# First layer of a feed-forward network for two blocks of tokens at once, with streamed sums of weights

## The chip, the core and the metric

The kernel runs on one core of one Trainium2 chip. The metric is the device time of one execution in microseconds (us). The core has five engines that run side by side, each through its own fixed list of instructions: PE (TensorE, the matrix engine; PEld is its loading of weights), DVE (VectorE), ACT (ScalarE), POOL (GpSimd) and SP (SyncE, which here only issues DMA transfers). Semaphores order them among each other.

## What is computed

Attention over 8 batches of 8 heads, 576 positions and 64 dimensions, in which scores more than tau below the largest of their row are dropped; its output, as 4608 tokens of 512 columns, goes through a network with one hidden layer of 2048. All in float32.

```python
scores = scale * np.matmul(q, k.transpose(0, 1, 3, 2))
thresh = np.max(scores, axis=-1, keepdims=True) - tau
scores = np.where(scores >= thresh, scores, -1000000000.0)
attn = softmax(scores)                      # in the reference written out
x = (attn @ v), heads side by side          # 4608 x 512
h = x @ w_in                                # 512 x 2048
out = (h * (1.0 / (1.0 + np.exp(-1.702 * h)))) @ w_out
```

## The kernel before, in words

**Attention.** Two heads make a pair, four pairs a batch, 32 pairs in all (n = 0 to 31). For a pair, PE multiplies keys and queries into scores (`scores`, L571), ACT copies them to SBUF (`keep`, L588), DVE takes maxima (`in_groups`, L594, `over_tiles`, L603), ACT crosses the halves (L613), DVE spreads the maximum (L620, L631) and subtracts it (`sub`, L658), ACT drops what is too small (`mask`, L664) and takes exponentials (`exps`, L668), in five tiles. DVE adds them up (L594 again); the sums are inverted (L742), written to DRAM (`sums_out`, L748), and read back spread over partitions (`sums_in`, L755). PE multiplies with the values (`values`, L679), and `place_x` (L783) writes the product with the inverse sums to a tile `xT` of tokens. From pair 6 on, the values of one pair and the scores of the next are one unbroken stretch of PE, a *run* of 144 recorded instructions. A run starts only when three PSUM buffers of the pool psA are free, and, before the change, when all five tiles of exponentials are there.

**Feed-forward.** The tokens are cut into 18 blocks of 256. Blocks 0 and 1 are computed plainly and together, 256 columns to a matmul (L838, L820). Blocks 2 to 13 use Strassen's scheme in Winograd's form, seven products in place of eight, for both layers. `seven` (L1699) lays the first layer of one block out: each quarter product P1 to P7 (`product1`, L895) is 2 halves of 4 x 2 matmuls with 128 columns, because the tokens of the block are halved (`BLK` 256, `HT` 128). Its left sides are quarters of `w_in` or sums of them, `wc[0..2]`, 1 MB each, made once and kept in SBUF (`w_copy`, `w_plus`, L871 and L875); its right sides are quarters of `xT` or sums of them (`x_sum`, L882). ACT and DVE add the products up (`keep1` L920, `add1` L924) and apply the activation (`silu1` L932). `second` (L1776) does the same for the second layer with 256 columns a matmul (`product`, L1230). Blocks 14 to 17 (`tail_blocks`, L1457) use the scheme twice, two blocks at a time; for that, sums of weights are made ahead, by `extra_sum` (L1015) and `extra2_sum` (L1102) in blocks 4 to 10, and stored in DRAM (L1023, L1110), from where they are streamed in.

**The order of the work.** The kernel plans its own order. Each step is a `task` with an engine, an estimated length, a rank, what it waits for and which buffers it takes and gives back; `run_in_order` (L245) plays the tasks through and writes every engine's instructions in the order in which they start there. Tables of numbers (`EARLY`, `SECOND`, `LATER`, `CV`, `L_RANK`, `W_RANK`) shift the ranks. On PE attention goes ahead of feed-forward as soon as it can start. What comes out is a fixed order; on the chip each engine keeps to it and waits where something is late. DMA transfers are issued by SP in the order of its list, one waiting behind another; a few are issued by POOL: the rows of the first eight pairs, `w_plus` and `t_plus` (L954), all ahead of 275 us.

**Buffers.** `arena2` holds scores, values and query/key tiles; its end, from the seat of `s_m1` on (`spare2`), holds `wc` and the sums of x while `seven` runs. `spare_g` (in `arena`) holds the second layer's sums of activations `s1` and `s2`, and for a moment the sums that `extra_sum` makes. The inverse sums of pairs from 6 on share one buffer, `mb`, with the maxima.

Of the kernel before, what the change touches and what calls it, by code (L numbers as in the profile page):

```python
# [10 lines left out]
FP32 = mybir.dt.float32  # L11
# [6 lines left out]
ALU = mybir.AluOpType  # L18
# [3 lines left out]
P = 128  # L22
# [10 lines left out]
def kernel(  # L33
# [94 lines left out]
    NXT = 5  # L128
    limits = {"psA": 3, "psM": 2, "s_m0": 4, "s_m1": 4, "s_t0": 1, "s_t1": 1, "io": 2, "hs": 2, "osb": 2, "xT": NXT, "mb": 1,
              "raw0": 1, "raw1": 1, "qkT0": 1, "qkT1": 1, "v_m0": 1, "v_m1": 1, "w64_0": 1, "w64_1": 1, "row": 1, "row_s": 1, "rc": 1}  # L130
    for x in ("raw0", "raw1", "qkT0", "qkT1", "mb"):
# [6 lines left out]
        "cross_max": -48.44,  # L138
        "exps": 8.27,
        "in_groups": -20.58,  # L140
        "keep": -91.91,
        "load_qk": -140.68,
        "load_v": -22.28,
        "mask": 10.76,
        "one_row": -86.85,
        "over_halves": -24.87,
        "over_tiles": -88.47,
        "place_x": -38.02,
        "row_in": 3.21,
        "row_out": -7.31,  # L150
        "scores_run": -131.23,
        "spread_max": 29.73,
        "spread_sums": 7.58,
        "sub": -0.95,
# [3 lines left out]
        "turned": -73.29,  # L158
# [3 lines left out]
        "cross_max": 21.33,  # L162
        "cross_sums": 28.0,
        "exps": -7.59,
        "in_groups": 89.35,
        "keep": 7.69,
        "load_qk": -3.13,
        "load_v": 156.87,
        "mask": 62.12,
        "over_halves": -25.79,  # L170
        "over_tiles": 12.47,
        "place_x": -6.25,
        "prep": 141.1,
        "row_in": 11.9,
        "row_out": 159.53,
        "scores_run": -65.52,
        "spread_max": 4.94,
        "sub": 100.98,
        "sums_in": 1.57,
        "sums_out": 102.83,  # L180
        "turn_rows": -12.68,
        "turn_sums": -7.39,
        "values": -29.52,
    }
    LATER = {
        "cross_max": 26.13,
        "cross_sums": -42.19,
        "exps": -10.12,
        "in_groups": -7.73,
        "keep": -14.9,  # L190
        "load_qk": -20.4,
        "load_v": -0.04,
        "mask": -16.94,
        "over_halves": 48.55,
        "over_tiles": -87.61,
        "place_x": -5.16,
        "prep": 102.89,
        "scores_run": -94.88,
        "spread_max": 11.06,
        "sub": 15.63,  # L200
        "sums_in": 16.82,
        "sums_out": 139.32,
        "turn_sums": -0.18,
        "values": 4.3,
# [3 lines left out]
        "cv_low": 87.73,  # L208
        "cv_power": 34.31,
        "cv_power2": 17.48,  # L210
        "cv_round": -2.96,
        "cv_whole": 74.25,
        "load_w": -29.8,
# [6 lines left out]
    TABLES, LOAD = {"exps": 1, "first_act": 1, "silu1": 2, "silu2": 2}, 1.28  # L220
# [144 lines left out]

    def seat(tag, x=0):
        o, size = room[tag][x]
        return arena2[:, o : o + size]
# [18 lines left out]
    def rc_pool(n):  # L387
        return "mb" if n >= SINGLE - 1 else "rc"
# [400 lines left out]
    hidden, acc, ths, osbs = {}, {}, {}, {}  # L789
# [14 lines left out]

    def tanh(j):
        ths[j] = work.tile([P, BANK], FP32, name="th", tag="io", bufs=2)
        nc.scalar.activation(out=ths[j], in_=hidden[j], func=AF.Tanh, scale=GELU_SCALE / 2)
# [80 lines left out]
    places = {}  # L888

# [66 lines left out]
    def quarters(blk):  # L956
        if blk < TAIL:
            return qas
        two_slots = [slot_of[f, blk % 2] for f in range(2)]
        return [[y[:, :, ts(h, HT)] for y in two_slots] for h in range(2)]  # L960
# [35 lines left out]
    assert room["s_m1"][0][0] >= N_G + 9 * BANK  # L996
    extra_rows = [dram.tile([P, 3 * BANK], FP32, name=f"ext{x}", tag=f"ext{x}", bufs=1) for x in range(7)]
    loose, tiles2 = {}, {}

    def loose_io(key):  # L1000
        if key not in loose:
            loose[key] = work.tile([P, BANK], FP32, name="th", tag="io", bufs=2)
        return loose[key]
# [11 lines left out]
    def extra_sum(x, k):  # L1015
        y = left1(x)
        a11, a12, a21, a22 = (y[:, c, ts(f, BANK)] for f in range(2) for c in range(2))
        u1, u2, u4 = (spare_g[:, ts(z, BANK)] for z in range(3))
        o, a, b, op = ((u1, a21, a22, ALU.add), (u2, u1, a11, ALU.subtract), (u4, a12, u2, ALU.subtract))[k]
        nc.vector.tensor_tensor(out=o, in0=a, in1=b, op=op)  # L1020

    def extra_out(x):
        nc.sync.dma_start(out=extra_rows[x], in_=spare_g[:, 0 : 3 * BANK])  # L1023

# [6 lines left out]
    def extra_in(blk, x, k):  # L1031
        if blk == TAIL and x == P2 and "b" not in loose:
            loose["b"] = work.tile([P, NDC, BLK], FP32, name="xT", tag="xT", bufs=NXT).rearrange(
                "p c t -> p (c t)"
            )
# [65 lines left out]

    def extra2_sum(x, k):  # L1102
        y = right2(x)
        b11, b12, b21, b22 = (y[:, ts(c, 4), ts(n, HT)] for c in range(2) for n in range(2))
        u1, u2, u4 = (four(spare_g[:, ts(z, BANK)]) for z in range(3))
        o, a, b = ((u1, b12, b11), (u2, b22, u1), (u4, b21, u2))[k]
        nc.vector.tensor_tensor(out=o, in0=a, in1=b, op=ALU.subtract)

    def extra2_out(x):
        nc.sync.dma_start(out=extra2_rows[x], in_=spare_g[:, 0 : 3 * BANK])  # L1110
# [218 lines left out]
    W_RANK = (-72.29, -7.42, 1.49, 46.38, 3.78, 10.04)  # L1329
# [40 lines left out]
    def first_blocks():  # L1370
        xs = list(placed.values())[-NPAIR:]
        for j in range(NFC):
# [7 lines left out]
            a = task("ACT", 0.48, FIRST, tanh, j, after=ffn[-1:], take=("io",))  # L1380
            gelus[j] = task("DVE", 0.59, FIRST, gelu_0, j, after=[a], give=("psM", "io"))
# [56 lines left out]
    queued = {"ch": [], "p5": []}  # L1438
# [337 lines left out]
    def second(blk, ready, sums, minus):  # L1776
# [4 lines left out]
        for x, p in order:  # L1781
# [19 lines left out]
            if p in (0, 2):  # L1801
                continue
# [279 lines left out]
```

## Time and profile before

| | |
|---|---|
| median of 3 runs (lowest, highest) | 1248.26 us (1247.51, 1250.88) |
| the profiled execution: its time, its span | 1251.82 us, 1250.0 us |
| mean granted clock of PE | 0.998 |
| read from and written to DRAM | 86.28 MB, 20.60 MB |

The span is the time from the first to the last instruction in the profile; some 2 us of the execution lie around it. In a line of the profile, L908 is line 908 of the kernel above; `out<-in` are the program's names of tiles, then partitions and tile shape, and `x32` the number of instructions that stand together or were grouped. PE's float32 matmul is recorded as two instructions, so the counts of the profile are twice those of the program. Start times count from the start of the span. A group's "mean ns" on PE contains the overlap of pipelined matmuls: pace is read from start to start or as busy time over count.

### The profile page before, as it was taken

The numbers are of one execution on the slowest core, as the hardware profiler recorded it, in microseconds if no ns is written. First come the engines' busy times: TensorE is split into PE (matmuls) and PEld (weight loads), VectorE is DVE, ScalarE is ACT, GpSimd is POOL, SyncE is SP. The second block draws the span as 40 slices with busy tenths as digits, with TensorE's granted clock in tenths as the row PEclk, the third lists the DMA queues.
The fourth block names the chain that finished last, engine by engine and source line by source line (L and its number), as shares of the span: only waits on it lengthen the run. The fifth ranks groups of instructions, "written<-read, shape, count | busy, mean of one in ns | idle before, by whom it ended". The sixth has DMA issues, their size and how long they took to land.

```text
span 1250.0 us, 27210 instructions
## 1 busy us (share of the span) xinstructions
PE 1222.6 (98%) x11264; PEld 1005.3 (80%) x11264; DVE 1085.7 (87%) x1683; ACT 827.7 (66%) x1209; POOL 32.6 (3%) x59
## 2 busy tenths in 40 slices
PE   8979999999999999999999999999999999999998
PEld 6636854487888888887979788888888897999998
DVE  6989997779879998999898998989788789999796
ACT  6999988786766766676767667667667586330430
POOL 0000012110000000000000000000000000000000
PEclk9999999999999999999999999999999999999999
DMA  8724458781313332223323241422221212344443
GB/s 244 189 68 112 140 126 140 145 152 43 72 39 97 68 91 66 79 65 74 92 57 99 46 116 42 116 49 66 44 71 22 64 45 72 114 120 140 144 121 100
DMA packets 187180, 117.05 MB, mean 94 GB/s; under 512 B 145392, under 2 KB 155632, under 8 KB 186928
## 3 DMA queue, kind: packets, MB, share of 16 engines
q1 hardware_dynamic: 179776, 103.93, 31.6%
q0 software_dynamic: 6592, 11.09, 5.1%
q8 instruction: 88, 1.44, 0.5%
q10 hardware_dynamic: 688, 0.30, 0.1%
q14 instruction: 36, 0.29, 0.1%
HBM read 86.28 MB, written 20.60 MB: 85 GB/s over the span
## 4 chain that ended last, share of the span: by engine, by line
PE 74%; DVE 12%; ACT 10%; DMA 3%; issue 1%; POOL 0%; SPq 0%; DVEq 0%; ACTq 0%; POOLq 0%
PE ops L1230 24%; PE hps L908 14%; PE ps L908 10%; PE pv L679 9%; PE ps L571 9%; ACT arena L668 3%; PE hps L1074 3%; DVE arena L1091 2%; ACT arena L664 2%; ACT arena L588 2%; PE ps L1074 2%; PE ps L1191 2%; DVE arena L1149 2%; PE ops L1191 1%; DVE part L594 1%
## 5 line engine op out<-in xcount | busy, mean ns | idle before, releaser
L594 DVE TRANSPOSE_TENSOR_REDUCE part<-arena 128x36 f32<-128x1152 f32 x300 | 365.8, 1242 | 62.4 <-ACT arena L588 50.0
L588 ACT COPY arena<-ps 128x576 f32<-128x576 f32 x288 | 170.6, 642 | 93.3 <-PE ps L571 93.2
L664 ACT ACTIVATE arena<-arena 128x1152 f32<-128x1152 f32 (+1 forms) x160 | 165.8, 1060 | 56.9 <-DVE arena L658 56.9
L668 ACT ACTIVATE arena<-arena,shift,scl 128x1152 f32<-128x1152 f32 (+1 forms) x160 | 196.6, 1247 | 1.9
L658 DVE TENSOR_TENSOR arena<-arena 128x1152 f32<-128x1152 f32 (+1 forms) x158 | 189.2, 1228 | 1.2 <-DMA arena<-row 0.3
L571 PE MATMUL ps<-arena 64*64 64x288 f32 x2304 | 171.5, 409 | 6.2 <-ACT arena L588 6.1
L1230 PE MATMUL ops<-w_out,arena 128*128 128x256 f32 x768 | 175.8, 382 | 0.0
L1230 PEld LDWEIGHTS ops<-w_out,arena 128*128 128x128 f32 x768 | 143.3, 190 | 27.3 <-issue 9.2
L679 PE MATMUL pv<-arena 64*64 64x288 f32 x2176 | 159.2, 405 | 0.0
L571 PEld LDWEIGHTS ps<-arena 64*64 64x64 f32 x2304 | 83.1, 133 | 66.9 <-ACT arena L588 25.7
L1230 PE MATMUL ops<-arena 128*128 128x256 f32 x576 | 128.5, 379 | 0.0
L679 PEld LDWEIGHTS pv<-arena 64*64 64x64 f32 x2176 | 80.8, 133 | 53.5 <-issue 7.7
L1230 PEld LDWEIGHTS ops<-arena 128*128 128x128 f32 x576 | 109.3, 190 | 15.3 <-issue 0.4
L908 PE MATMUL hps<-xT,w_in 128*128 128x128 f32 x768 | 89.7, 275 | 0.0
L908 PEld LDWEIGHTS hps<-xT,w_in 128*128 128x128 f32 x768 | 88.6, 192 | 1.1 <-issue 0.5
L927 DVE TENSOR_TENSOR arena<-ps,arena 128x512 f32<-128x512 f32 x72 | 46.9, 679 | 44.0 <-PE ps L908 41.3
L922 ACT COPY arena<-hps 128x512 f32<-128x512 f32 x72 | 41.4, 575 | 39.4 <-PE hps L908 39.3
L838 PE MATMUL hps<-xT,w_in 128*128 128x256 f32 x256 | 56.1, 380 | 0.0
L820 PE MATMUL ops<-w_out,arena 128*128 128x512 f32 x128 | 55.9, 595 | 0.0
L838 PEld LDWEIGHTS hps<-xT,w_in 128*128 128x128 f32 x256 | 48.4, 190 | 7.8 <-issue 0.9
L1088 ACT COPY arena<-hps 128x512 f32<-128x512 f32 x38 | 22.2, 583 | 47.7 <-PE hps L1074 47.7
L613 ACT ACTIVATE other<-red,minus_gap 32x18 f32<-32x18 f32 x118 | 36.2, 307 | 25.0 <-DVE red L603 23.4
(211 smaller groups left out, 1773.3 us busy)
## 6 DMA issues: line engine op xcount, KB each, us to landing
arena<-in_v_dram SPq DMA_DIRECT2D x128, 144.0 KB
arena<-exu SPq DMA_DIRECT2D x42, 256.0 KB
arena<-ext SPq DMA_DIRECT2D x39, 256.0 KB
out_dram<-osb SPq DMA_DIRECT2D x32, 256.0 KB
arena<-in_q_dram SPq DMA_DIRECT2D x112, 72.0 KB
arena<-in_k_dram SPq DMA_DIRECT2D x112, 72.0 KB
arena<-row_s SPq DMA_DIRECT2D x48, 144.0 KB
w_out<-in_moe_w_in_dram SPq DMA_DIRECT2D x12, 512.0 KB
```

The costliest lines, as they stand in the source:

```text
L571: nc.tensor.matmul(ps[ts(c, KT), h, 0:SH], lhsT=mats[n, 1][ts(h, D), ts(j, KT)], rhs=mats[n, 0][ts(h, D), ts(c, SH)], start=True, stop=True,)
L588: nc.scalar.copy(out=sT[n, t][:, u], in_=pss.pop((n, j))[:, :, 0:SH])
L594: nc.vector.tensor_reduce(out=stats[n, op][:, t * 2 * QB : min(2 * t + 2, NK) * QB], in_=sT[n, t].rearrange("p u h (g d) -> p (u h g) d", ...
L658: engine.tensor_tensor(out=s, in0=s, in1=mbs[n].unsqueeze(1).to_broadcast(list(s.shape)), op=ALU.subtract)
L664: nc.scalar.activation(out=s, in_=s, func=AF.Prelu, alpha=STEEP)
L668: nc.scalar.activation(out=s, in_=s, func=AF.Exp, scale=scl, bias=shift)
L679: nc.tensor.matmul(o[c][ts(h, D), 0:SH], lhsT=left(j, h)[ts(c, KT)], rhs=sT[n, t][ts(c, KT), u, h, :], start=(j == 0), stop=(j == NK - 1),)
L820: nc.tensor.matmul(acc[i], lhsT=g0[:, j, ts(i, P)], rhs=w_out[:, j, :], start=(j == 0), stop=(j == NFC - 1),)
L838: nc.tensor.matmul(hidden[j][:, ts(i, BLK)], lhsT=w_in[:, c, ts(j, P)], rhs=xTs[i][:, c, :], start=(c == 0), stop=(c == NDC - 1),)
L908: nc.tensor.matmul(o[:, ts(j, HT)], lhsT=left[:, c, ts(4 * y + j, P)], rhs=right[:, c, :], start=(x in (P1, P2, P5) and j + c == 0), stop= ...
L1074: nc.tensor.matmul(o[:, ts(j, HT)], lhsT=left[:, ts(j, P)], rhs=right, start=(m in (P1, P2, P5) and j == 0), stop=(j == 3), skip_group_che ...
L1230: nc.tensor.matmul(banks[blk][k][:, ts(o, HM)], lhsT=left[:, j, :], rhs=right[:, j, :], start=(j == 0), stop=(j == HF - 1),)
```

## The change

Blocks 7 and 8, 9 and 10, 11 and 12 get their first layer together (`seven4`): the scheme's two halves of tokens are then two whole blocks of 256, so each matmul has 256 columns instead of 128, and a product is four quarters of 2 x 2 matmuls, two quarters at a time. The second layer stays as it was, block after block. The larger tiles take the room of `wc`: the three sums of weights are copied to DRAM (`keep_wc`, SP) after block 2's weights are ready, fetched in 256 KB pieces by POOL into four turns of `spare_g` (`w_flow`), and copied back whole before block 13 (`sums_back`), which is done by `seven` again. A fifth turn waits until the first has been used.

The sums for the tail are made in blocks 3 to 6 (eight of them, in a tile of `xT`) and in 7, 9 and 11 (six, through the one buffer `scrap`, each addition waiting for the store before it). `xT` has six buffers instead of five, and the activation's tile of blocks 0 and 1 and some tail tiles come from that pool. Inverse sums of pairs 16 to 27 get a buffer of their own, `rc2`. A run of the pairs after 16 may begin when two of the five tiles of exponentials are there; each further tile is waited for inside the run. The tables of rank shifts have new numbers. A function `alone` for a block 8, 10 or 12 by itself is added too; no block uses it.

```diff
-    NXT = 5
+    NXT = 6
+    SECOND_RC = 4 * NPAIR
     def seat(tag, x=0):
+        if tag == "rc2":
+            return spare2[:, ds(N_G + 4 * BANK, S)]
...
     def rc_pool(n):
+        if SECOND_RC <= n < NP - NPAIR:
+            return "rc2"
         return "mb" if n >= SINGLE - 1 else "rc"
...
+    WIDE = 7
+    WIDE_AT = (7, 9, 11)
+    g1 = spare2[:, 0:N_G].rearrange("p (f j t) -> p f j t", f=2, t=BLK)
+    scrap = spare2[:, ds(N_G + 3 * BANK, BANK)]
...
+    def keep_wc(x):
+        for c in range(2):
+            nc.sync.dma_start(
+                out=wrows[x].rearrange("q p (c f) -> p c q f", c=2)[:, c],
+                in_=wc[x][:, c, :].rearrange("p (q f) -> p q f", q=4),
+            )
...
+    def w_in_turn(k):
+        return spare_g[:, ts(k % 4, BANK)]
+
+    def w_flow(k, x, q):
+        nc.gpsimd.dma_start(out=w_in_turn(k), in_=wrows[WC_OF[x]][q])
...
+    def product4(blk, q, x, k):
+        y = q % 2
+        b11, b12, b21, b22 = (xTs[blk + h][:, ts(d, 2), :] for d in range(2) for h in range(2))
+        right = (b11, b21, x3[1], b12, x3[2], x3[0], b22)[x]
+        if x in WC_OF:
+            left = w_in_turn(k).rearrange("p (c f) -> p c f", c=2)
+        else:
+            left = left1(x)[:, :, ts(q, 2 * P)]
...
+        o = bank1(x, y)
+        for j in range(2):
+            for c in range(2):
+                nc.tensor.matmul(
+                    o[:, ts(j, BLK)], lhsT=left[:, c, ts(j, P)], rhs=right[:, c, :],
+                    start=(x in (P1, P2, P5) and j + c == 0), stop=(j + c == 2),
+                    skip_group_check=True,
+                )
...
+    def scrap_out(second, x, k):
+        nc.sync.dma_start(out=(extra_rows, extra2_rows)[second][x][:, ts(k, BANK)], in_=scrap)
...
+    EARLY_EXTRAS = {
+        3: ((0, P6), (0, P5)), 4: ((0, P3), (0, P1)), 5: ((0, P2), (1, P1)), 6: ((1, P2), (1, P6)),
+    }
+    LATE_EXTRAS = {7: ((0, P4), (1, P4)), 9: ((0, P7), (1, P7)), 11: ((1, P5), (1, P3))}
...
+    def seven4(blk):
...
+        freed = last1 + (kept_wc + list(extra_out_done.values()) if first else [])
...
+        for second_layer, x in LATE_EXTRAS[blk]:
+            for k in range(3):
+                a = task("DVE", 0.6, FIRST, scrap_sum, second_layer, x, k, after=freed + [t_ready[-1], a])
+                a = task("SP", 0.55, FIRST, scrap_out, second_layer, x, k, after=[a], take=RING[0])
+                a = transfer("DMS", 1.4, a, 2, give=RING[0])
...
+        flow_users = {k: ffn[-1:] if k > 1 else last5[-1:] for k in range(4)}
...
+        for (q, x), k in turn.items():
+            if k >= 4:
+                tasks[ready[q, x][0]][5].append(users[k - 4])
...
+            second(blk + h, {P1: both(0, h), P2: both(1, h), P4: both(1, h)}, sums, minus)
...
+    BEGUN = 2
...
-            elif next_blk >= FIRST7:
+            elif next_blk - 1 in WIDE_AT:
+                seven4(next_blk - 1)
+            elif next_blk == TAIL - 1:
+                sums_back()
+                seven(next_blk)
...
+            elif next_blk >= FIRST7 and next_blk not in WIDE_AT:
                 seven(next_blk)
...
-                    after=exped[m] + [loaded[m], pq, pk] + after if t == 0 else [a],
+                    after=exped[m][: BEGUN if n > SECOND_RC else NKT + 1] + exped[m][NKT + 1 :] + [loaded[m], pq, pk] + after
+                    if t == 0 else [a, exped[m][t]],
```

More of the change, by code (lines that the diff above doesn't have):

```diff
@@ L1379, in first_blocks @@
                 ))
-            a = task("ACT", 0.48, FIRST, tanh, j, after=ffn[-1:], take=("io",))
-            gelus[j] = task("DVE", 0.59, FIRST, gelu_0, j, after=[a], give=("psM", "io"))
+            a = task("ACT", 0.48, FIRST, tanh, j, after=ffn[-1:], take=("io",) + (("xT",) if j == 0 else ()))
+            gelus[j] = task("DVE", 0.59, FIRST, gelu_0, j, after=[a],
+                give=("psM", "io") + (("xT",) if j == NFC - 1 else ()),
+            )
         plain1[:] = ffn[-1:]
@@ L1491, in tail_blocks @@
                     after=[extra_out_done[x]] + ([a, placed[NP - NPAIR]] if where == "b" else []),
-                    take=RING[0] + (("xT", "io", "io") if where == "b" and k == 1 else ()),
+                    take=RING[0] + (("xT", "xT") if where == "b" and k == 1 else ()),
                 )
@@ L1774, with sums_back @@
+    def sums_back():
+        outs = list(extra_out_done.values()) + list(extra2_out_done.values())
+        a = None
+        for x in (P6, P5, P3):
+            after = ffn[-1:] + [a] + (last1 + outs if x == P3 else [])
+            a = task("SP", 1.1, FIRST, back_wc, WC_OF[x], after=after, take=RING[0])
+            wc_back[x] = transfer("DMS", 5.6, a, 2, give=RING[0])
+            w_done[{P6: 1, P5: 0, P3: 3}[x]] = wc_back[x]
+    last5, seated = [], []
     T_OF = {P6: 2, P7: 4, P4: 3, P5: 1}
```

449 lines of the change are left out of this document (348 added, 101 removed).

## The prediction

> **What bounds the kernel now.** I read the page's first part, then the busy time by stages, then the order of TensorE's instructions in time, and last what stands just ahead of the attention runs.
>
> ```profile
> PE 1222.6 (98%) x11264; PEld 1005.3 (80%) x11264; DVE 1085.7 (87%) x1683; ACT 827.7 (66%) x1209; POOL 32.6 (3%) x59
> ```
>
> TensorE is busy for 98% of the span. Where the other 27 us lie is told by two stages, from the first block of the seven-product kind to the last of them, and from there to the end (columns: length, then busy time and count for PE, PEld, DVE, ACT, POOL, then clock, DMA share, GB/s):
>
> ```profile
> 256.00:1057.00 801.00, 801.00 (x7343) 675.71 (x7342) 700.59 (x1002) 551.05 (x793) 3.10 (x2) 1.00 0.28 69
> 1057.00:1250.00 193.00, 185.38 (x1645) 179.90 (x1643) 166.60 (x362) 54.35 (x105) 0.00 (x0) 1.00 0.42 126
> ```
>
> In the first stage, which holds blocks 2 to 13, TensorE has no gap at all in 801 us, at full clock. In the tail it lacks 193.0 - 185.4 = 7.6 us, so about 27.4 - 7.6 = 20 us are lost ahead of 256 us. The change works inside the first stage. There a wait taken away gains nothing, because none reaches TensorE; only fewer or faster matmuls gain, and every new wait of TensorE costs its full length.
>
> A busy engine need not be at its best pace, so the pace is read from starts:
>
> ```profile
> 1020.84 3.74 PE L908 MATMUL ps<-xT,arena 128*128 128x128 f32 x32
> 1024.42 7.07 PE L1230 MATMUL ops<-w_out,arena 128*128 128x256 f32 x32
> 1031.33 1.89 PE L1230 MATMUL ops<-arena 128*128 128x256 f32 x8
> ```
>
> The 32 first-layer instructions of 128 columns (two to one float32 matmul of the program) take 1024.42 - 1020.84 = 3.58 us, or 111.9 ns each; the 32 of 256 columns take 1031.33 - 1024.42 = 6.91 us, or 215.9 ns each. Two of 128 columns cost 223.8 ns and one of 256 does the same work in 215.9.
>
> **The change part by part.** *Matmuls.* Blocks 7 to 12 run their first layer as three pairs. A block has 7 products of 2 halves of 4 x 2 matmuls, 112 matmuls in two pairs of halves or 224 recorded instructions; a whole block by itself agrees:
>
> ```profile
> 850.00:900.00 50.00, 25.17 (x224) 25.17 (x224) 1.00 0.23 53
> 550.00:600.00 50.00, 24.87 (x112) 21.04 (x112) 1.00 0.32 82
> ```
>
> (first row line L908 alone, second line L1230 alone). Six blocks are 1344 instructions of 128 columns, which become 672 of 256. The saving is 672 x (223.8 - 215.9) = **5.3 us**. Its bounds: by the whole-stage rows a pair costs 2 x 25.17/224 = 224.7 ns and a 256 one 24.87/112 = 222.1, breaks for attention included, which leaves 672 x 2.7 = 1.8 us. I take 5.3, since the first layer of the plain blocks is the same form with the same weights and holds the pace over its whole run:
>
> ```profile
> L838 PE MATMUL hps<-xT,w_in 128*128 128x256 f32 x256 | 56.1, 380 | 0.0
> ```
>
> 56.1/256 = 219 ns, its breaks included. TensorE's second layer, attention and tail are the same instructions as before.
>
> *Streamed weight sums.* The three summed weights (1 MB each) are copied to DRAM once after block 2 has made them, come back in 36 pieces of 256 KB on GpSimd's queue, twelve to a pair of blocks, and whole before block 13. No row shows such a piece; the nearest are smaller and larger transfers of the same queue (last number: median us to landing):
>
> ```profile
> arena<-row_s POOLq DMA_DIRECT2D x8, 144.0 KB, 5.1
> arena<-w_out POOLq DMA_DIRECT2D x3, 1024.0 KB, 9.9
> ```
>
> So a piece lands 5.1 to 9.9 us after its issue; I take 5.6, near the 144 KB row. GpSimd's issue is bounded by
>
> ```profile
> 250.18 1.24 POOL L877 DMA_DIRECT2D arena<-w_in  x1 [1.09 <-PE ps L571]
> ```
>
> at 1.24 us each, and nothing else is on that queue by then. The first piece of a pair may start when the P5 product of the block before has read its buffer. Behind that stand P3 and the four tasks of P1 and P2: six tasks of 8 x 215.9 = 1.73 us, 10.4 us of cover against 1.2 + 5.6 = 6.8. The later ones reuse a buffer after P6 and are read at P3: seven tasks, 12.1 us, and in the new order of instructions an attention run stands between as well. Cost 0; at the upper end, 1.2 + 9.9 = 11.1, TensorE would wait 0.7 us a pair, 2 us in all.
>
> *Copies out and back.* Six issues on SP for each direction. Back, they wait for block 12's last product; block 13's P1 (16 matmuls, 3.6 us), an attention run and P2 (3.6 us) stand in the new order ahead of P6, which needs the first of them, 16 us; a 1 MB transfer took 9.9. Cost 0, and 1 us if three share the queue. On the way out they stand in SP's queue ahead of the q and k loads of two later head pairs, in a stretch where the DMA engines are already busy:
>
> ```profile
> 250.00:300.00 50.00, 49.97 (x440) 41.18 (x433) 40.92 (x63) 35.56 (x55) 4.34 (x3) 1.00 0.66 120
> ```
>
> 3 MB at 120 GB/s are 25 us of that queue; the loads are for a run a whole interval (28 us or more, below) on. Cost 0 to 2 us, I take 0.
>
> *Sums for the tail.* The same 42 additions and the same bytes as before, but in 34 stores instead of 14; the last 18 sums share one buffer, so each addition waits on VectorE for the store before it, and behind it waits whatever VectorE has next. Before, SP stood waiting for them and TensorE did not:
>
> ```profile
> SPq L1110 <- DVE arena L1107: 48.4, 7, 9.6
> ```
>
> Cost 0 as long as VectorE has room (third rival).
>
> *x sums.* Eight VectorE subtractions of 256 columns a pair of blocks become four of 512:
>
> ```profile
> L886 DVE TENSOR_TENSOR arena<-xT,arena 128x256 f32<-128x256 f32 x24 | 10.0, 418 | 0.1
> L1107 DVE TENSOR_TENSOR arena<-arena 128x512 f32<-128x512 f32 x9 | 6.1, 677 | 0.2
> ```
>
> 8 x 0.42 - 4 x 0.68 = 0.6 us less a pair on VectorE, hidden under TensorE: 0. ScalarE's copies and SiLUs keep count and size; its program has 32 table loads instead of 28.
>
> *Own buffer for the reciprocal sums; runs begun after two of five exponentials.* Both can only start attention runs sooner. TensorE has no gap there, so they are worth 0 by themselves. But they are needed. Before, runs come at 28.1 and 39.5 us by turns, the long turn holding the first layer:
>
> ```profile
> 646.10 2.09 ACT L668 ACTIVATE arena<-arena,shift,scl 128x1152 f32<-128x1152 f32 x2
> 649.01 1.20 PE L679 MATMUL pv<-arena 64*64 64x288 f32 x16
> 679.86 0.87 ACT L668 ACTIVATE arena<-arena,shift,scl 128x576 f32<-128x576 f32 x1
> 688.53 1.20 PE L679 MATMUL pv<-arena 64*64 64x288 f32 x16
> ```
>
> The run at 649.01 starts 0.8 us after its last exponential ends (648.2). The next one's exponentials end at 680.7, 31.7 us after that start, and have 7.8 us to spare. In the new order two runs in a first layer of a pair stand 14 tasks (24.2 us) and a run (9.0) apart, 33.2 us: 1.5 us to spare, plus what beginning early gives. The scores' copies of the run stand behind the exponentials on ScalarE and three PSUM buffers hold the scores, so a run can go on some 3.4 us (seven of its eighteen half-microsecond steps) without the last exponential. Cost 0, with 4.9 us of margin in place of 7.8.
>
> *Start and tail.* The new order of TensorE up to the first seven-product block differs only by two matmuls on the other side of a run, and the tail's by where the last run of values stands (after its first instead of its fourth product) and small swaps. The tail's gaps are 7.6 us; I take no change, and 1.5 us either way.
>
> **Sum.** The profiled execution took 1251.8 us (span 1250.0); less 5.3 gives 1246.5. It lies 3.6 us above the median of the runs, 1248.3; measured against that, 1248.3 - 5.3 = **1243.0 us**.
>
> **Rivals.** *The pace of the new matmuls is that of the broken stage.* Saving 1.8 us, 1246.5. For it: the stage rows; against it: unbroken runs of 215.9 ns with two kinds of weights.
>
> *The change hides its gain behind late weights.* VectorE is busy almost without a break in the short interval:
>
> ```profile
> 620.90:649.00 28.10, 28.10 (x233) 21.95 (x232) 27.81 (x40) 19.32 (x26) 0.00 (x0) 1.00 0.15 36
> 649.00:688.50 39.50, 39.50 (x393) 34.86 (x392) 33.02 (x50) 27.07 (x42) 0.00 (x0) 1.00 0.39 104
> L594 DVE TRANSPOSE_TENSOR_REDUCE part<-arena 128x36 f32<-128x1152 f32 x300 | 365.8, 1242 | 62.4 <-ACT arena L588 50.0
> ```
>
> If GpSimd can write a transfer's descriptors only between two VectorE instructions, the issue waits up to one of 1.24 us. With the slowest landing that is 1.24 + 1.2 + 9.9 = 12.3 against 10.4: 2 us on each of three pairs, 6 us, 1249. Against it: at 250.18 GpSimd issued in 1.24 us beside VectorE. The Trainium skill ("SBUF — State Buffer", the box on the "DVE blocks DMA" trap) speaks against this change at this place: while VectorE runs an instruction that takes both ports, GpSimd cannot write descriptors, with 620 ns growing to about 3100 in its example. By that page's 2.5 us instead of 1.24 the estimate would be 3.2 us a pair, some 10 us, and no gain.
>
> *VectorE and ScalarE fall behind in the pairs (the other side).* A block takes VectorE 27.81 + 33.02 = 60.8 of 67.6 us; two blocks 121.7 of the 133.4 us that a pair then lasts, so 11.7 us are free. Six of the one-buffer sums fall in each pair. In the new order as few as three VectorE rows, some 3 us, stand between two of them; with a store that lands like the 5.1 us row and half a microsecond of issue each sum waits 2.6 us, 16 us a pair. That is 4 us over what is free, and two of the four table loads added fall in the same stretches:
>
> ```profile
> L668 ACT ACT_TABLE_LOAD x13 | 16.7, 1283 | 0.2
> ```
>
> 4 + 2 x 1.28 = 6.6 us a pair, 20 us in all less the 5.3 gained: 1263. It decides from 11.7 us of waits a pair on; up to there it costs nothing, and at 16 it makes the kernel slower even without the loads (3 x 4.3 = 13 against 5.3: 1256). For it: margins of 4.9 us in place of 7.8; against it: no sum made VectorE wait long enough before to reach TensorE.
>
> **How the numbers follow.** The forecast has 0.60; its own range is 1241.5 to 1244.5 by start and tail. The broken pace has 0.12 (1246.5); late weights 0.08 (1245 to 1249); VectorE behind 0.15 (1250 to 1263); 0.05 is for a gain over 7 us by a better start or tail. This kernel's measurement can tell about 0.3%, 3.7 us, from no change: faster is below 1244.5, slower above 1252.0. Faster: 0.52 of the forecast's 0.60, and 0.05 of the larger gain, with 0.03 from the mixed cases, 0.60. Slower: 0.13 of the last rival, 0.01 of late weights, 0.14. Same: 0.26. The range of 1239.5 to 1252.5 leaves out the worse part of the last rival and the end of the larger gain.
>
> **What would show it.** The 256-column first-layer rows at 216 ns from start to start and 672 of them; still no gap of TensorE between 256 us and the tail, the tail starting near 1052; no wait of TensorE on the streamed weights; runs in the pairs about 33 us apart. Wrong would be: TensorE waiting at product P6 for a DMA, at a run's later tiles for ScalarE's exponentials, or VectorE waiting on the stores of its sums for more than 11.7 us a pair.

## The result, and the profile after

Measured in alternation on one chip, the changed kernel takes 1245.13 us (median of 8 runs, 1244.32 to 1245.79) and the kernel before 1250.32 us (8 runs, 1247.51 to 1251.22). The ratio is 0.9958, with a 95% interval of 0.9949 to 0.9967: faster by 0.42%, or 5.2 us. The forecast was 1243.0 us from a median of 1248.3, a ratio of 0.9958 too; the 2.1 us between 1243.0 and 1245.13 are the other median of the kernel before. The profiled execution took 1244.32 us (span 1242.5). Of the 7.5 us between the two profiled executions some 2.3 are chance, since the one of before lay 1.5 us above its median and the one of after 0.8 below.

In the kernel after, the lines have moved: scores L577, values L685, score copies L594, exponentials L674, maxima and sums L600, `place_x` L789, first layer of one block L918, of a pair of blocks L1060 (`product4`), second layer L1354, the tail's first layer L1208 with its additions L1225 and its x sums L1180, its second layer L1315, the streamed pieces L1037 (`w_flow`).

The page's first part and two stages of the profile after (length, then busy time and count for PE, PEld, DVE, ACT, POOL, then clock, DMA share, GB/s):

```profile
PE 1218.3 (98%) x10592; PEld 979.3 (79%) x10592; DVE 1083.4 (87%) x1671; ACT 827.8 (67%) x1213; POOL 52.0 (4%) x95
```

```profile
256.00:1052.40 796.40, 795.91 (x6652) 650.03 (x6651) 697.69 (x990) 553.33 (x802) 22.59 (x38) 1.00 0.35 89
...
1052.00:1242.50 190.50, 184.33 (x1643) 179.36 (x1641) 166.48 (x363) 50.89 (x101) 0.00 (x0) 1.00 0.43 126
```

TensorE has 11264 - 10592 = 672 instructions fewer, as it should. The middle stage still has next to no gap (0.5 us in 796); the tail now has 6.2 us of them instead of 7.6. The stretch of a pair's first layer, in order of time (start, duration, and the number of instructions that stand together):

```profile
636.32 3.72 PE L1060 MATMUL ps<-arena,arena 128*128 128x256 f32 x16
639.88 3.62 PE L1060 MATMUL hps<-xT,w_in 128*128 128x256 f32 x16
643.33 3.62 PE L1060 MATMUL hps<-arena,w_in 128*128 128x256 f32 x16
646.78 3.62 PE L1060 MATMUL ps<-xT,arena 128*128 128x256 f32 x16
650.24 7.07 PE L1354 MATMUL ops<-w_out,arena 128*128 128x256 f32 x32
```

From start to start, 16 instructions take 3.45 us, 216 ns each: the forecast pace. The first row holds 0.1 us more (3.56); an attention run ends just ahead of it.

Adding up all of TensorE's starts by stage, each instruction counted until the next one starts, splits the 7.5 us of the two profiles:

| stage | before | after | difference |
|---|---|---|---|
| start, up to the first seven-product block | 256.37 | 253.55 | -2.82 |
| first layer of blocks 7 to 12 (before: half of that of blocks 2 to 13) | 150.55 | 147.41 | -3.14 |
| second layer of blocks 2 to 13 | 294.45 | 293.36 | -1.09 |
| attention in the middle stage | 205.83 | 207.52 | +1.69 |
| tail, to the end of the span | 192.25 | 190.06 | -2.19 |

(The other half of the first layer, 150.55 us before and 150.60 after, is not in the table.) The start varies from one execution to the next: it takes 253.5 to 255.1 us in the profiles of experiments 1, 2 and 4, which have the changed kernel's buffers and tables there, and 254.1 and 255.5 us in two variants of the kernel before (experiment 6). So its 2.8 us cannot be told from chance. The other stages repeat: from the first seven-product block to the tail it is 801.4 us in the kernel before and in both its variants of experiment 6, and 798.9 to 799.0 us in the changed kernel, in that of experiment 2 and in the changed kernel with the old order of the tail.

The gain of the wide matmuls is the second and third row together, 4.2 us: six of the attention runs that used to interrupt the second layer, about 0.2 us each, interrupt the wide first layer now, which moves 1.1 us from one row to the other. The other 1.1 of the 5.3 us are five short stops in the wide layer (at 609.6, 744.9, 746.8, 878.7 and 880.7 us, 0.17 to 0.28 us each), where a weight load waits for a copy or an addition of the products before it (L1101 and L1106 below). The waits of TensorE's weight loads, in the middle stage of the profile after (total us, times, longest):

```profile
PEld ps L577 <- ACT arena L594: 12.3, 35, 0.6
...
PEld ps L1060 <- ACT arena L594: 2.2, 5, 0.4
PEld hps L1060 <- ACT arena L1101: 1.0, 3, 0.4
...
PEld ps L1060 <- DVE arena L1106: 0.8, 2, 0.4
```

and the same of before:

```profile
PEld ps L571 <- ACT arena L588: 7.7, 23, 0.4
```

The waits of the scores (L577) on the score copies are longer and more frequent. Four runs, at 415.76, 446.05, 551.47 and 1024.14 us, hold 1.4 of attention's 1.7 us: they take 9.2 to 9.4 us where no run of the middle stage before took more than 8.97, and their weight loads wait 0.6 to 1.3 us for score copies. The five waits of L1060 on score copies stand behind attention runs and belong to the breaks. A weight load overlaps the matmul before it, so such totals are more than what TensorE loses.

### The profile page after: what moved, and what is told of

The parts are those of the page before. It is cut to its first block, busy times and chain, and to the rows that moved or that the text cites. A ratio compares the mean times of both kernels' runs of the same rounds, so it can differ in the third digit from the quotient of the medians.

```text
span 1242.5 us, 26030 instructions
## 1 busy us (share of the span) xinstructions
PE 1218.3 (98%) x10592; PEld 979.3 (79%) x10592; DVE 1083.4 (87%) x1671; ACT 827.8 (67%) x1213; POOL 52.0 (4%) x95
## 4 chain that ended last, share of the span: by engine, by line
PE 71%; ACT 16%; DVE 8%; DMA 2%; issue 1%; SPq 0%; POOL 0%; ACTq 0%; DVEq 0%
PE ops L1354 23%; PE ps L577 9%; PE pv L685 9%; PE hps L1060 7%; PE ps L1060 5%; ACT arena L674 4%; PE hps L850 4%; ACT arena L670 4%; PE hps L918 3%; PE hps L1208 3%; PE ps L918 3%; ACT arena L594 3%; DVE arena L1225 2%; PE ps L1208 2%; PE ps L1315 2%; DVE arena L1273 2%
## 5 line engine op out<-in xcount | busy, mean ns | idle before, releaser
L600 DVE TRANSPOSE_TENSOR_REDUCE part<-arena 128x36 f32<-128x1152 f32 x300 | 364.9, 1240 | 64.6 <-ACT arena L594 49.1
L594 ACT COPY arena<-ps 128x576 f32<-128x576 f32 x288 | 170.6, 642 | 104.6 <-PE ps L577 104.4
L674 ACT ACTIVATE arena<-arena,shift,scl 128x1152 f32<-128x1152 f32 (+1 forms) x160 | 195.4, 1247 | 1.8
L577 PE MATMUL ps<-arena 64*64 64x288 f32 x2304 | 171.6, 409 | 5.8 <-ACT arena L594 5.4
L1354 PE MATMUL ops<-w_out,arena 128*128 128x256 f32 x768 | 174.6, 381 | 0.1
L1354 PEld LDWEIGHTS ops<-w_out,arena 128*128 128x128 f32 x768 | 144.2, 190 | 25.6 <-issue 5.7
L685 PE MATMUL pv<-arena 64*64 64x288 f32 x2176 | 160.2, 407 | 0.0
L577 PEld LDWEIGHTS ps<-arena 64*64 64x64 f32 x2304 | 81.2, 132 | 69.4 <-ACT arena L594 31.5
L685 PEld LDWEIGHTS pv<-arena 64*64 64x64 f32 x2176 | 81.3, 133 | 53.8 <-issue 9.1
L1354 PE MATMUL ops<-arena 128*128 128x256 f32 x528 | 118.1, 379 | 0.0
L1354 PEld LDWEIGHTS ops<-arena 128*128 128x128 f32 x528 | 100.2, 190 | 14.0 <-issue 0.4
L850 PEld LDWEIGHTS hps<-xT,w_in 128*128 128x128 f32 x256 | 48.4, 190 | 7.8 <-issue 1.3
L1222 ACT COPY arena<-hps 128x512 f32<-128x512 f32 x38 | 22.2, 584 | 48.1 <-PE hps L1208 48.1
L832 PEld LDWEIGHTS ops<-w_out,arena 128*128 128x128 f32 x128 | 24.1, 190 | 30.1 <-issue 29.8
L918 PEld LDWEIGHTS hps<-xT,w_in 128*128 128x128 f32 x384 | 44.3, 192 | 0.7 <-issue 0.5
L918 PE MATMUL hps<-xT,w_in 128*128 128x128 f32 x384 | 44.8, 275 | 0.0
L1037 POOL DMA_DIRECT2D arena<-wrow x36 | 19.5, 541 | 599.5 <-DVE arena L664 301.7
```

Source lines behind the costliest of these rows:

```text
L577: nc.tensor.matmul(ps[ts(c, KT), h, 0:SH], lhsT=mats[n, 1][ts(h, D), ts(j, KT)], rhs=mats[n, 0][ts(h, D), ts(c, SH)], start=True, stop=True,)
L594: nc.scalar.copy(out=sT[n, t][:, u], in_=pss.pop((n, j))[:, :, 0:SH])
L600: nc.vector.tensor_reduce(out=stats[n, op][:, t * 2 * QB : min(2 * t + 2, NK) * QB], in_=sT[n, t].rearrange("p u h (g d) -> p (u h g) d", ...
L674: nc.scalar.activation(out=s, in_=s, func=AF.Exp, scale=scl, bias=shift)
L685: nc.tensor.matmul(o[c][ts(h, D), 0:SH], lhsT=left(j, h)[ts(c, KT)], rhs=sT[n, t][ts(c, KT), u, h, :], start=(j == 0), stop=(j == NK - 1),)
L832: nc.tensor.matmul(acc[i], lhsT=g0[:, j, ts(i, P)], rhs=w_out[:, j, :], start=(j == 0), stop=(j == NFC - 1),)
```

## The experiments

All medians and ratios of this part are against runs of the kernel before on the same chip, in alternation with it.

**1. Is it the pace?** The changed kernel with each wide matmul issued as two of 128 columns.

```diff
-                nc.tensor.matmul(
-                    o[:, ts(j, BLK)], lhsT=left[:, c, ts(j, P)], rhs=right[:, c, :],
+                for t in range(2):
+                    nc.tensor.matmul(
+                        o[:, ds(j * BLK + t * HT, HT)], lhsT=left[:, c, ts(j, P)], rhs=right[:, c, ts(t, HT)],
...
```

> The changed kernel in which each 256-column matmul of the pairs is issued as two of 128 columns; everything else (streamed weights, buffers, ranks, begun runs) stays. If the pace of the matmuls is the gain, the first layer of blocks 7 to 12 goes from 147.4 us back to 150.5 and the breaks stay: 672 x 7.9 ns = 5.3 us longer, 1250.4 us, ratio 1.000 to the kernel before. If the new order around them is the gain (the tail's gap of 2 us that is gone, and the start), most of it stays: 1247 us or less, ratio 0.9975 or less.

Measured: 1249.87 us (11 runs), ratio 1.0000 (0.9991 to 1.0009). In time order (its L1061 is the pairs' first layer):

```profile
642.52 3.74 PE L1061 MATMUL hps<-xT,w_in 128*128 128x128 f32 x32
646.10 3.74 PE L1061 MATMUL hps<-arena,w_in 128*128 128x128 f32 x32
```

The same work takes 3.58 us where the wide form takes 3.45, and by starts the pairs' first layer is back at 151.5 us against 147.4. All the rest of the change is still in this kernel, and it gains nothing: the pace is the net gain. Whether the wide form is faster in the matmul or because it needs half the weight loads (the 1344 of this kernel against 672) is not shown, since both change together. (Its attention in the middle stage, +1.7 us, and its tail, -2.2 us, both moved as in the changed kernel, and nearly cancel.)

**2. Do the streamed weights come in time?** Each 256 KB piece is fetched twice, one behind the other.

```diff
-        nc.gpsimd.dma_start(out=w_in_turn(k), in_=wrows[WC_OF[x]][q])
+        for _ in range(2):
+            nc.gpsimd.dma_start(out=w_in_turn(k), in_=wrows[WC_OF[x]][q])
```

> The changed kernel with every 256 KB piece of the weight sums fetched twice into the same place (72 transfers instead of 36). If the cover of 10.4 us holds as reckoned, a piece that lands 3.0 us after an issue of 0.54 us, done twice in a row, is still there in time: 1245 us, ratio 0.996, no wait of TensorE on it. If the weights are late already and only just hidden, each pair of blocks loses about 3 us: 1254 us, ratio 1.003.

Measured: 1244.25 us (5 runs), ratio 0.9955 (0.9942 to 0.9967), no slower than the changed kernel. Its middle stage, and then its row of DMA issues (number, size, median us to landing):

```profile
256.00:1052.00 796.00, 795.53 (x6653) 649.65 (x6652) 696.90 (x988) 553.84 (x802) 41.63 (x74) 1.00 0.39 101
```

```profile
arena<-wrow POOLq DMA_DIRECT2D x72, 256.0 KB, 3.1
```

GpSimd is busy nearly twice as long (41.6 us in place of 22.6), and TensorE still lacks only 0.5 us. So the rival of late weights falls.

**3. Are begun runs worth nothing?** The changed kernel with runs planned only when all five tiles of exponentials are there.

```diff
-    BEGUN = 2
+    BEGUN = NKT + 1
```

> The changed kernel in which a run waits for all five tiles of exponentials again. The planner puts the runs elsewhere: the last values come some 12 us of feed-forward work later than in the changed kernel. If early starts are worth nothing by themselves because TensorE always has other work, the stage of blocks 2 to 13 keeps its length and the whole is 1245 to 1247 us, ratio 0.996 to 0.9975. If the pairs need the early start, TensorE gets gaps at the runs or at the tail's start: over 1250 us, ratio over 1.000.

Measured: 1288.67 us (4 runs), ratio 1.0308 (1.0293 to 1.0322). "Worth nothing" fell by far: 43 us. TensorE's instructions in time, with the idle time ahead and who ended it:

```profile
975.45 0.72 PE L577 MATMUL ps<-arena 64*64 64x288 f32 x8
984.94 1.23 PE L685 MATMUL pv<-arena 64*64 64x288 f32 x6 [8.78 <-ACT arena L674]
...
996.09 1.24 PE L577 MATMUL ps<-arena 64*64 64x288 f32 x8 [6.03 <-ACT arena L594]
997.10 2.14 PE L685 MATMUL pv<-arena 64*64 64x288 f32 x16
999.02 2.15 PE L577 MATMUL ps<-arena 64*64 64x288 f32 x16
...
1092.86 1.20 PE L685 MATMUL pv<-arena 64*64 64x288 f32 x16 [3.94 <-ACT arena L674]
1097.98 4.13 PE L685 MATMUL pv<-arena 64*64 64x288 f32 x40 [3.92 <-ACT arena L674]
1111.72 2.05 PE L1208 MATMUL hps<-arena 128*128 128x128 f32 x8 [9.60 <-DVE arena L1180]
```

The instructions themselves wait for the same data as before; the switch acts only through the plan. In the first pair of blocks two runs now stand 50.8 us apart (592.99 and 643.75) where the changed kernel has 35.2, so attention falls behind by part of a run; it is made up by two runs back to back at 967 us, the second of which stands waiting for its exponentials, and by last values 13.6 us into the tail. By starts, attention takes 367.0 us in place of 326.2 and that is 41 of the 43 us.

**4. Is the own buffer of the reciprocal sums needed?** `rc2` is taken away, so the sums share `mb` again.

```diff
     def rc_pool(n):
-        if SECOND_RC <= n < NP - NPAIR:
-            return "rc2"
         return "mb" if n >= SINGLE - 1 else "rc"
```

> The changed kernel in which the inverse sums of pairs 16 to 27 share the buffer of the maxima again. If the own buffer only starts runs sooner, it is worth nothing: 1245 us, ratio 0.996. If the shared buffer holds the maxima of the next pair back long enough to reach TensorE, 2 us or more: 1247 us or more, ratio over 0.9975.

Measured: 1253.27 us (7 runs), ratio 1.0026 (1.0016 to 1.0037): 8 us lost, and more than the gain. **And if all runs are begun early?** The changed kernel with begun runs from pair 9 on:

```diff
-                    after=exped[m][: BEGUN if n > SECOND_RC else NKT + 1] + exped[m][NKT + 1 :] + [loaded[m], pq, pk] + after
+                    after=exped[m][: BEGUN if n > SINGLE + 1 else NKT + 1] + exped[m][NKT + 1 :] + [loaded[m], pq, pk] + after
```

> The changed kernel with begun runs for all unbroken runs from pair 9 on, not only after pair 16; it computes all. Theory (where TensorE has no gap an earlier run is worth nothing, and it pays only where the next exponentials are the last to come): 1245, within 1.5 us. Rival A (a run begun early waits inside itself for its later exponentials, and those waits are TensorE's): slower by 0.5 us or more a run, 8 runs, 1249 or more. Rival B (it also draws attention out of the tail, as the kernel without begun runs pushed it in): 1240 to 1243.

Measured: 1255.46 us (5 runs), ratio 1.0043 (1.0029 to 1.0056). The time is in Rival A's range, but not for its reason: the eight runs that now may begin early, at 281.63 to 512.58 us, take 8.96 to 8.97 us each, so none of them waits inside. The time is lost in runs behind them, at 619.97 to 930.41 us, which may begin early in the changed kernel too and do not wait there. Both kernels lose the same 9 us in attention (335.2 us in each, against 326.2). TensorE's waits in the middle stage, first without `rc2` (its lines are two lower), then with all runs begun:

```profile
PE pv L683 <- ACT arena L672: 5.8, 3, 1.9
```

```profile
PE pv L685 <- ACT arena L674: 3.9, 2, 1.9
PE ps L577 <- ACT arena L594: 2.3, 4, 0.7
PE hps L918 <- ACT arena L932: 1.1, 1, 1.1
```

In both, the pairs' runs stand unevenly: 26.4, 31.8, 36.0 and 42.9 us apart with all begun (697.45, 723.88, 755.72, 791.75, 834.64), where the changed kernel has 31.6 to 35.2. The run at 755.72 comes 58.3 us after the last but one, waits, and takes 11.45 us in place of 8.97; without `rc2` the run at 756.63 does the same after 58.3 us. In the changed kernel two intervals are never under 65 us there, and no run of the pairs waits. This fits a chain of maxima, masks and exponentials that needs more than 58.3 us for two pairs; that chain was not changed by itself.

**5. Are the new numbers of the planner's tables part of it?** The changed kernel with all the old numbers (one of some 80 lines):

```diff
     LATER = {
-        "cross_max": 86.38,
+        "cross_max": 26.13,
...
```

> The changed kernel with the old tables of rank shifts (EARLY, SECOND, LATER, CV, L_RANK, W_RANK); it computes all. Theory (the gain is the pace of 672 matmuls, and the tables only keep the order such that nothing is late): in the planned order the runs now come irregularly and the last run of values stands 11.6 us of feed-forward work later in the tail, as it also did in the kernel without begun runs, so it loses: 1255 to 1270. Rival (the new numbers are worth nothing, since TensorE has no gap ahead of the tail): 1245, as the changed kernel, within 2 us. Second rival (the new numbers are the gain): about 1250.

Measured: 1269.34 us (4 runs), ratio 1.0155 (1.0141 to 1.017). And the kernel before with all the new ones, the same lines the other way round:

> The kernel before with the new tables of rank shifts and nothing else; it computes all, with first layers of 128 columns. Theory (the gain is the pace of the wide matmuls): no gain is possible from them, 1250 or more; in the planned order the last two runs merge and the last values stand later, so rather 1252 to 1265. Rival (a better order is a large part of the gain): 1245 to 1248.

Measured: 1286.57 us (4 runs), ratio 1.0293 (1.0277 to 1.0309), slower still than was expected. TensorE's waits of the two (changed kernel with old numbers, then kernel before with new ones) show the same two places, late last exponentials and the tail behind them:

```profile
PE hps L1208 <- DVE arena L1180: 8.7, 1, 8.7
PE pv L685 <- ACT arena L674: 8.6, 3, 4.3
PE ps L577 <- ACT arena L594: 7.2, 12, 1.0
```

```profile
PE pv L679 <- ACT arena L668: 13.7, 2, 10.9
...
PE hps L1074 <- DVE arena L1046: 8.4, 1, 8.4
```

In these runs each set of numbers is good only with its own shape of the first layer.

**6. What shortened the tail?** In the tail's first layer TensorE waits four times for VectorE in the kernel before, 1.9 us together, and twice after the change, 0.8 us (total us, times, longest; first before, then after):

```profile
PE hps L1074 <- DVE arena L1091: 1.1, 3, 0.4
PE ps L1074 <- DVE arena L1091: 0.8, 1, 0.8
```

```profile
PE hps L1208 <- DVE arena L1225: 0.8, 2, 0.4
```

Buffers and order were tried. First the six `xT` buffers alone, with the activation's and the loose tail tiles in that pool, in the kernel before:

```diff
-    NXT = 5
+    NXT = 6
...
-        ths[j] = work.tile([P, BANK], FP32, name="th", tag="io", bufs=2)
+        if "th" not in places:
+            places["th"] = x_home()
+        ths[j] = places["th"][:, ts(j % 2, BANK)]
...
```

> The kernel before with six xT buffers in place of five, and the activation's tile and the loose tail tiles in that pool, as in the changed kernel; it computes all, in the same order on TensorE. The changed kernel's tail is 2.2 us shorter, and a wait of TensorE on VectorE of 1.6 us at 1076 us is gone from it. Theory A (the buffers did that): the wait goes, 1248.0 to 1248.5. Theory B (the place of the last run of values, after the first in place of the fourth tail product, did that): the wait stays, 1250, within 0.7 us.

Measured: 1250.34 us (11 runs), ratio 1.0001 (0.9992 to 1.001), with the wait still there. So the buffers are not what shortened the tail. Then the order of the tail, in both directions, by a chain over its first 24 pieces in the planner:

```diff
+    TAIL_ORDER = [(0, 0), "v", (0, 1), (0, 2), (0, 5), (1, 0), (0, 3), (1, 1), (1, 2), (0, 4),
...
+    chain = [pv_last if y == "v" else which[("product2", TAIL) + y] for y in TAIL_ORDER]
+    for a, b in zip(chain, chain[1:]):
+        tasks[b][5].append(a)
     run_in_order()
```

> The kernel before with the first 24 pieces of TensorE's tail (23 products and the last run of values) put in the order that the changed kernel has there, the last values after the first product in place of the fourth; all ahead of it stays, and it computes all. Theory B (the place of the last values and its neighbours is the whole of the tail's 2.2 us): the wait of TensorE at 1076 us goes and the tail's first layer takes 89.7 us in place of 91.5: 1248.2. Theory A (the tail ran better in the changed kernel for what lies ahead of it, sums and loads that come earlier): 1250, or more, since the last exponentials would now be late by up to 2 us.

Measured: 1254.72 us (5 runs), ratio 1.0043 (1.003 to 1.0055): worse than the kernel before.

> The changed kernel with the first 24 pieces of TensorE's tail in the order of the kernel before (last values after the fourth product); it computes all. Theory B: the wait of 1.8 us comes back, 1246.9. Theory A: 1245.1, as the changed kernel.

Measured: 1245.89 us (8 runs), ratio 0.9971 (0.9961 to 0.9981). Of the 1.8 us only 0.9 come back (the tail's first layer takes 90.5 us, against 89.7 in the changed kernel and 91.5 before), with a wait of 0.4. So Theory B falls: the order alone makes the old kernel worse, and is worth half of it in the new one. What else there is stands on VectorE; here are the last inversion of sums, the first `place_x` of the last pair, and TensorE's start after the wait, in the kernel before, where the tail starts at 1057.75:

```profile
1063.98 0.27 DVE L742 RECIPROCAL flat_s<-red 128x18 f32<-128x18 f32 x1
...
1071.05 0.94 DVE L783 TENSOR_TENSOR xT<-pv,arena 128x64 f32<-128x64 f32 x4
...
1077.09 1.16 PE L1074 MATMUL ps<-xT,th 128*128 128x128 f32 x8 [0.77 <-DVE arena L1091]
```

in the changed kernel, where it starts at 1052.44:

```profile
1056.13 0.27 DVE L748 RECIPROCAL flat_s<-red 128x18 f32<-128x18 f32 x1
...
1065.27 0.94 DVE L789 TENSOR_TENSOR xT<-pv,arena 128x64 f32<-128x64 f32 x4
```

and in the kernel before with the new order of the tail, where it starts at 1056.91:

```profile
1063.13 0.27 DVE L742 RECIPROCAL flat_s<-red 128x18 f32<-128x18 f32 x1
...
1069.33 0.95 DVE L783 TENSOR_TENSOR xT<-pv,arena 128x64 f32<-128x64 f32 x4 [2.10 <-DMA arena<-row_s]
...
1073.46 1.16 PE L1074 MATMUL ps<-xT,arena 128*128 128x128 f32 x8 [3.23 <-DVE arena L1091]
```

The last inversion comes 6.2 us after the tail's start in both kernels with the old plan, and 3.7 us after it in the changed one (and 3.7 in the changed one with the old tail order, 1056.22 against 1052.54). The inverse sums then go to DRAM and back before `place_x` and the tail's sums of x can go on, and TensorE's early products wait behind those. With the new order on the old plan VectorE stands 2.10 us for these sums, and TensorE 3.23 us behind it: there the late inversion costs. That it is the other half of the tail's gain fits the four kernels, but is not shown: the inversion was not moved by itself, and in the kernel before VectorE's wait just ahead of this `place_x`, 2.37 us up to 1070.44, ended with a copy of ScalarE (L1088) and not with the sums.

**7. Can attention's 1.7 us be had back?** The changed kernel with the old numbers of the one table `LATER` for head pairs 8 to 15:

```diff
+    LATER_OLD = {
...
-            biases = EARLY if a[0] < NPAIR else SECOND if a[0] < 2 * NPAIR else LATER
+            biases = EARLY if a[0] < NPAIR else SECOND if a[0] < 2 * NPAIR else LATER_OLD if a[0] < 16 else LATER
```

> The changed kernel with the old numbers of the table LATER for head pairs 8 to 15 and the new ones after; it computes all. In the planned order the runs of blocks 2 to 6 then stand as before the change, and those of the pairs as in the changed kernel. The attention runs of the middle stage took 1.7 us more in the changed kernel, in runs at 378, 416, 446 and 551 us. Theory (those 1.7 us are the price of where the new numbers put these runs, a term of the change by itself): 1243.6 to 1244.4. Rival (they are the price of begun runs): 1245.1, no change.

Measured: 1243.56 us (5 runs), ratio 0.9956 (0.9942 to 0.997). By the ratio it cannot be told from the changed kernel (0.9958). In its trace the runs at 414.4 and 442.5 us take 8.91 and 8.97 us again (the changed kernel has 9.38 and 9.25 at 415.8 and 446.1), and the attention of the middle stage takes 206.7 us instead of 207.5. So about half of the 1.7 us is where the new numbers put these runs. Most of the other half stands in the runs at 549.37 and 1022.21, which still take 9.37 and 9.19 us; no cause was tried for these, and the gain is too small for the times to show.

## Why the prediction was right

**The pace** was the term that mattered, and it was right: 216 ns a wide instruction against 223.8 for two narrow ones, and with the pace undone the gain is gone. The sum took all of 5.3 us; by starts 4.2 arrived, in two places. The 1.1 us short are the five stops of the wide layer on copies and additions of its own products, for which the working had no term. The breaks for attention runs cost the same in either layer and cancel.

**Streamed weights, 0:** right, with the sizes off on the safe side. Issue and landing by the profile after, the line of `w_flow`:

```profile
L1037 POOL DMA_DIRECT2D arena<-wrow x36: 539/539/595, 578.7 to 895.4; - x36
...
DMA to landing us min/median/max: 2.7/3.0/4.7
```

0.54 us to issue and 3.0 to land, against the 1.24 and 5.6 that I took; the slowest landing was 4.7, so the cover of 10.4 us was never near. VectorE did not hold the issues up: none of the 36 took more than 0.6 us, in a stretch where VectorE was busy for 295.5 of 347 us. By the Trainium skill ("SBUF — State Buffer", the box on the "DVE blocks DMA" trap) GpSimd cannot write descriptors while VectorE runs an instruction that takes both ports, and the estimate from that page's figures was 10 us lost. No such loss shows here. Whether any VectorE instruction of this stretch takes both ports, no run here shows, so the rule itself is not refuted.

**VectorE behind in the pairs:** did not come. VectorE's waits in the pairs' stretch of the profile after, 583 to 930 us, are all on ScalarE and TensorE, and none on a store of a sum:

```profile
DVE part L600 <- ACT arena L594: 20.9, 20, 4.3
DVE arena L1106 <- PE ps L1060: 18.9, 7, 5.7
DVE part L600 <- ACT arena L674: 5.0, 3, 4.3
DVE osb L1376 <- PE ops L1354: 3.1, 2, 1.8
```

**Own buffer and begun runs, "worth 0 by themselves", but needed:** the second half of that step was right and its margin of 4.9 us was too large. The runs in the pairs come 31.6 to 35.2 us apart, as forecast (33.2). Of the run at 660.69 the last exponentials, on ScalarE in the profile after, read

```profile
656.38 4.57 ACT L674 ACTIVATE arena<-arena,shift,scl 128x1152 f32<-128x1152 f32 x4
```

and end at 660.95, 33.6 us after the run before started at 627.35; the prediction had 31.7 and 1.5 us to spare. By its 3.4 us for beginning early, 3.1 us of margin were left in place of 4.9. The run has already begun by then, 0.26 us earlier: without the right to begin, it would be planned elsewhere. Taking that right away cost 43 us in experiment 3, and taking the own buffer away 8 us in experiment 4. The first half of the step, worth 0 by themselves, was not tried in the kernel before. What I did not see at all is that such an edit acts through the plan: a run of the pairs that may not start does not wait a little, it changes places. The debt is paid in the runs behind it (all 9 us of experiment 4) and in the tail (which is 22.6 us longer in experiment 3).

**Start and tail, 0 ± 1.5:** here the sum was right by two errors that cancel. The tail gave 2.2 us, which I had taken as 0, and attention in the middle stage took 1.7, which I had taken as 0 too, on the ground that the runs are the same instructions. They are, but a run has waits of its own on the score copies, and four runs stood where these were longer. The start's 2.8 us are little more than the 2.3 by which the two profiled executions differ by chance. So the mechanism was right and the number in part luck: 4.2 from the pace, 2.2 from the tail and -1.7 from attention make 4.7 us, in place of 5.3 from the pace alone, and the half microsecond up to the measured 5.2 is less than the start varies.

## What to carry to other kernels

In a stage where TensorE has no gap, count its instructions at the pace read from start to start, and expect that sum less the short stops on the work of other engines: 4.2 of 5.3 us here. Edits that only move work in a planned order are free there only as long as the runs still find their inputs ready; price them by what happens when one run loses its place (8 to 43 us here), not by the wait of a single run. Before a gain in the tail is put down to the order or to a buffer, measure when the last work of the stage before ends, counted from the tail's start.

## What the runs showed of the hardware

A long wait costs TensorE more than its length. In the kernel without begun runs, around the wait of 8.8 us at 976 us (columns as above; the clock is the third number from the end):

```profile
984.00:990.00 6.00, 4.59 (x24) 1.39 (x24) 4.78 (x6) 6.00 (x7) 0.00 (x0) 0.50 0.62 124
990.00:996.00 6.00, 0.06 (x4) 0.00 (x0) 5.96 (x10) 4.11 (x6) 0.00 (x0) 0.50 0.32 51
996.00:1000.00 4.00, 3.91 (x36) 2.05 (x40) 3.14 (x8) 0.67 (x2) 0.00 (x0) 0.50 0.03 5
1000.00:1003.00 3.00, 3.00 (x40) 1.67 (x36) 1.10 (x1) 1.28 (x2) 0.00 (x0) 0.66 0.35 98
1003.00:1006.50 3.50, 3.50 (x60) 1.72 (x52) 1.76 (x3) 2.36 (x4) 0.00 (x0) 1.00 0.00 0
```

TensorE ran dry at 976.2 us, and the granted clock fell to 0.50 some 2 us later, at 978.2. It stayed there until 1002.0, some 6 us after the second of the long waits had ended at 996.09. At 0.50, 16 attention matmuls took 1.92 us (997.10 to 999.02 in experiment 3) where they take 0.97 otherwise. The two runs back to back took 21.9 us more than at full pace; the waits in them are 15.3 us (8.78, 6.03 and two short ones), so 6.6 us more were lost. The 76 instructions that started at half clock, 59 ns slower each, make 4.5 of them; where the other 2 went is not shown. The Trainium skill ("TensorE: Matmul & The Clock Gate", Part 1) states half the clock after an idle window of about 3.4 us, and full clock after about as long of sustained work. The halving agrees with these rows; the times differ, 2 us of idleness before it and 6 us of work before full clock here.

The 256 KB loads from DRAM that GpSimd issued landed in 3.0 us (median), less than the 5.4 us of its 144 KB loads from `row_s` in the same profile. So size did not order these two transfers. The loads from `row_s` stood in another stretch, before 256 us, so what did is not shown.
